# Turning nine of twenty normalized blocks by DMA, and a re-planned order, in a two-layer linear-attention and gated-MLP kernel

## The chip, the cores and the metric

One core of a Trainium2 chip runs the whole program. TensorE (PE in the profile) multiplies, VectorE (DVE) and ScalarE (ACT) read its results out of PSUM, GpSimd (POOL) works on SBUF alone, and SyncE (SP) and ScalarE issue the DMAs. The metric is the device time of one execution in microseconds (us). Less is better.

## The reference

`x` is 2048 rows of 512 in bf16. Two layers follow one another with the same weights; each adds an attention part A and a gated part B to `x`, each behind a layer normalization without weights:

```python
qkv = (x @ wqkv).reshape(B, S, 3, H, Dh)          # H = 32 heads of Dh = 16
pq, pk = q @ w_phi, k @ w_phi                      # per head, 16 x 16
phi_q = concat([softmax(pq), softmax(-pq)])
phi_k = concat([softmax(pk), softmax(-pk)])
kv, z = phi_k^T @ v, sum(phi_k)                    # sums over all 2048 rows
A = ((phi_q @ kv) / (phi_q @ z + 1e-6)) @ wo
B = (relu(x @ W_gate) * (x @ W_up)) @ W_down       # 1376 wide
```

No row of an attention output can be made before `kv` and `z` are summed over all rows.

## The kernel before

**Tiling.** The 2048 rows are 16 tiles of 128 rows, taken in five blocks of 2, 4, 4, 4 and 2 tiles (`SLABS`). Layer L (0 or 1) and block s have a normalization for part A, called `aLs`, and one for part B, called `gLs`: twenty in all.

**Stages of a block.** `layernorm` takes the statistics of each tile on VectorE (line 730, 731), makes the factor on ScalarE as exp(-0.5 ln) (733, 735), applies it on VectorE (750) or ScalarE (747) into `ytile`, and turns rows into columns, `yT`, which is what all following matmuls read. Two ways of turning exist: one tile at a time (`tr`, line 612) where `STEPS` says so, and else `strips` (line 775): four PSUM banks, 16 matmuls of 32x32 blocks a tile against an identity, and four evictions from PSUM by VectorE (690) or ScalarE (693). `keys` makes `expk` = exp(+-k) (803), its sums `Zk` (805), the reciprocal `rZk` (807), `vhat` = v times the reciprocal (815) on GpSimd or VectorE, and the products `kv` (827). `queries` makes `expq` (871). `attend` makes denominators (886 to 902), spreads the result over the partitions, either through TensorE (973, blocks 0 and 1) or through a scratch in device memory (DMAs of lines 912 and 916, blocks 2 to 4), scales `expq` by it (958, 988, 991), forms the numerators (928) and multiplies by `wo`. `glu` is part B; its outputs are added to `x_sb` at line 995.

**The order.** The program is recorded as a list of operations with a cost each. `Program.schedule` then places them: at each step it takes, among the operations whose inputs are ready, the one with the earliest start less a bonus (`BONUS`, by stage), and among those the lowest place in the list less a lead (`LEAD`, by stage). `ENG` says which engine takes an operation that more than one could do. The result is one fixed order for each engine, with semaphore waits between engines; at run time an engine executes its list in order and waits where its next operation isn't ready. The planner's costs decide the order and nothing else: they hold no engine up at run time. An operation with `port=True` is kept by the planner from lying beside a GpSimd operation.

**Queues.** SP issues the loads, then the scratch DMAs, then the stores of the output, in one list; ScalarE issues two key weight loads and one small one at the start.

Of the kernel before, what the change touches and what calls it, by code (L numbers as in the profile page):

```python
# [20 lines left out]
LEAD = {'': 1581,  # L21
 'at00': -9,
 'at01': -1074,
 'at02': -507,
 'at03': -757,
 'at10': -335,
 'at11': 762,
 'at12': -656,
 'at13': 331,
 'at14': -567,  # L30
 'd00': -5820,
 'd01': -1699,
 'd02': -13878,
 'd03': -2622,
 'd04': 3155,
 'd10': -13359,
 'd11': -2460,
 'd12': -1931,
 'd13': 71,
 'd14': -310,  # L40
 'fk': -480,
 'gl00': -2522,
 'gl01': 1205,
 'gl02': -5857,
 'gl03': -1218,
 'gl04': 504,
 'gl10': -2926,
 'gl11': -481,
 'gl12': -7344,
 'gl13': -46,  # L50
 'gl14': -166,
 'k00': 4572,
 'k01': 869,
 'k02': 459,
 'k03': -281,
 'k04': -136,
 'k10': 388,
 'k11': -124,
 'k12': -1352,
 'k13': 414,  # L60
 'k14': -1,
 'la00': -523,
 'la01': -375,
 'la02': 9240,
 'la03': 2125,
 'la04': -103,
 'la10': -743,
 'la11': -3565,
 'la12': -1372,
 'la14': 7230,  # L70
 'lg00': 199,
 'lg01': -221,
 'lg02': 153,
 'lg04': -687,
 'lg11': -282,
 'lg12': -264,
 'lg13': 794,
 'lg14': 2775,
 'nm00': 842,
 'nm01': 32,  # L80
 'nm02': 3263,
 'nm03': -579,
 'nm04': 406,
 'nm10': -741,
 'nm12': 16,
 'nm13': -1558,
 'nm14': -3291,
 'q00': 5078,
 'q01': -515,
 'q02': -692,  # L90
 'q03': 3551,
 'q04': -1249,
 'q10': -241,
 'q11': -69,
 'q12': -281,
 'q13': -2355,
 'q14': -138,
 'sp00': 803,
 'sp01': 206,
 'sp02': 643,  # L100
 'sp03': 36,
 'sp04': 2026,
 'sp10': 11,
 'sp11': -275,
 'sp12': -193,
 'sp13': -604,
 'sp14': 1242,
 'su0': -202,
 'su1': -6,
 'wo00': -564,  # L110
 'wo01': -1486,
 'wo02': -805,
 'wo03': -998,
 'wo04': 84,
 'wo10': 477,
 'wo11': 1154,
 'wo12': -216,
 'wo13': -222,
 'wo14': -8,
 'z00': -275,  # L120
 'z01': -232,
 'z02': -28,
 'z03': -803,
 'z04': 287,
 'z10': -247,
 'z11': 1911,
 'z12': 85,
 'z13': -5,
 'z14': 170}
BONUS = {'': 400,  # L130
 'at00': 1500,
 'at01': 400,
 'at02': 200,
 'at03': 200,
 'at04': 200,
 'at10': 400,
 'd03': 200,
 'd11': 800,
 'd12': 200,
 'fk': 400,  # L140
 'fq': 200,
 'gl03': 200,
 'gl04': 200,
 'gl11': 200,
 'gl12': 1500,
 'k12': 200,
 'la00': 400,
 'la01': 200,
 'la13': 200,
 'lg10': 400,  # L150
 'nm00': 200,
 'nm04': 200,
 'q11': 200,
 'sp00': 200,
 'sp01': 200,
 'sp03': 200,
 'sp10': 400,
 'sp11': 200,
 'sp13': 200,
 'su0': 800,  # L160
 'su1': 1500,
 'wo04': 400,
 'wo10': 400,
 'wo13': 200,
 'wo14': 200,
 'z03': 200,
 'z04': 200,
 'z10': 200,
 'z12': 400,
 'z13': 200}  # L170
HOLD = {}
ENG = {'ap/a00/0': 'act',
 'ap/a01/0': 'dve',
 'ap/a01/1': 'dve',
 'ap/a01/3': 'dve',
 'ap/a02/0': 'dve',
 'ap/a02/3': 'dve',
 'ap/a03/0': 'dve',
 'ap/a10/1': 'act',
 'ap/a11/1': 'act',  # L180
 'ap/a12/1': 'act',
 'ap/a12/2': 'act',
 'ap/a13/0': 'act',
 'ap/a13/3': 'act',
 'ap/a14/1': 'act',
 'ap/g01/0': 'act',
 'ap/g01/1': 'act',
 'ap/g01/3': 'act',
 'ap/g02/0': 'act',
 'ap/g02/3': 'act',  # L190
 'ap/g11/0': 'act',
 'ap/g12/2': 'act',
 'ap/g13/0': 'act',
 'ap/g13/2': 'act',
 'ap/g13/3': 'act',
 'ap/g14/1': 'act',
 'em/01/00': 'act',
 'em/01/01': 'dve',
 'em/01/02': 'act',
 'em/11/02': 'act',  # L200
 'em/11/03': 'dve',
 'fck3': 'act',
 'ftk0': 'dve',
 'ftq2': 'dve',
 'ftq3': 'dve',
 'ot/00/1': 'act',
 'ot/00/3': 'act',
 'ot/01/1': 'dve',
 'ot/01/2': 'dve',
 'ot/01/3': 'dve',  # L210
 'ot/02/1': 'dve',
 'ot/02/2': 'dve',
 'ot/02/3': 'dve',
 'ot/03/3': 'dve',
 'ot/04/1': 'dve',
 'ot/04/2': 'dve',
 'ot/04/3': 'dve',
 'ot/10/2': 'dve',
 'ot/11/1': 'dve',
 'ot/13/0': 'dve',  # L220
 'ot/14/0': 'dve',
 'ot/14/1': 'dve',
 'ot/14/2': 'dve',
 'vc/0/5': 'dve',
 'vc/0/6': 'dve',
 'vc/1/0': 'dve',
 'vc/1/12': 'dve',
 'vc/1/2': 'dve',
 'vc/1/5': 'dve',
 'vc/1/6': 'dve',  # L230
 'vc/1/7': 'dve',
 'vc/1/8': 'dve',
 'vc/1/9': 'dve',
 'vh/0/10/1': 'dve',
 'vh/0/13/1': 'dve',
 'vh/0/15/0': 'dve',
 'vh/0/15/1': 'dve',
 'vh/0/7/0': 'dve',
 'vh/0/9/0': 'dve',
 'vh/1/0/1': 'dve',  # L240
 'vh/1/1/0': 'dve',
 'vh/1/10/0': 'dve',
 'vh/1/14/1': 'dve',
 'vh/1/15/0': 'dve',
 'vh/1/15/1': 'dve',
 'vh/1/3/1': 'dve',
 'vh/1/4/1': 'dve',
 'vh/1/5/0': 'dve',
 'vh/1/8/1': 'dve',
 'yc/a01/01': 'act',  # L250
 'yc/a01/03': 'act',
 'yc/a02/00': 'act',
 'yc/a02/03': 'act',
# [3 lines left out]
 'yc/a04/1': 'dve',  # L257
 'yc/a10/00': 'dve',
 'yc/a10/02': 'dve',
 'yc/a11/03': 'act',  # L260
 'yc/a12/01': 'act',
 'yc/a12/03': 'act',
 'yc/a13/00': 'dve',
# [3 lines left out]
 'yc/g01/03': 'act',  # L267
 'yc/g02/00': 'dve',
 'yc/g04/00': 'dve',
 'yc/g04/02': 'dve',  # L270
 'yc/g04/03': 'act',
 'yc/g10/0': 'dve',
 'yc/g10/1': 'dve',
 'yc/g11/02': 'dve',
 'yc/g11/03': 'act',
 'yc/g12/01': 'act',
 'yc/g13/02': 'dve',
 'yc/g14/02': 'dve',
 'yc/g14/03': 'act'}
# [29 lines left out]
class Op:  # L309
    __slots__ = ("idx", "eng", "fn", "reads", "writes", "occ", "lat", "name", "is_dma", "nbytes",  # L310
                 "deps", "odeps", "users", "missing", "ready", "start", "finish", "cnt", "stream", "prio", "bonus", "port")

    def __init__(self, idx, eng, fn, reads, writes, occ, lat, name, is_dma=False, nbytes=0):
        self.idx, self.eng, self.fn = idx, eng, fn
        self.reads, self.writes = list(reads), list(writes)
        self.occ, self.lat, self.name = float(occ), float(lat), name
        self.is_dma, self.nbytes = is_dma, nbytes
        self.deps, self.odeps, self.users = set(), set(), []
        self.missing, self.ready = 0, 0.0
        self.start = self.finish = self.cnt = self.stream = None  # L320
        self.prio = idx
        self.bonus, self.port = 0.0, False


class Program:
# [4 lines left out]
    DMA_BW = 270.0  # L330

# [4 lines left out]
    def op(self, eng, fn, reads=(), writes=(), occ=100.0, lat=None, name="", bonus=0.0, port=False):  # L336
        o = Op(len(self.ops), eng, fn, reads, writes, occ, occ + 100.0 if lat is None else lat, name)
        o.bonus, o.port = bonus + BONUS.get(self.tag, 0.0), port
# [5 lines left out]
    def dma(self, eng, fn, reads=(), writes=(), nbytes=0, name=""):  # L344
        o = Op(len(self.ops), eng, fn, reads, writes, self.DMA_ISSUE[eng], 0, name, True, nbytes)
        o.bonus = BONUS.get(self.tag, 0.0)
        o.prio -= LEAD.get(self.tag, 0)
        self.stages.setdefault(self.tag, []).append(o)
        self.ops.append(o)
        return o  # L350
# [42 lines left out]
    def schedule(self):  # L393
        self.derive()
        free = {e: 0.0 for e in ENGINES}
        qfree = ported = 0.0
        ready = {e: [] for e in ENGINES}
# [9 lines left out]
        while left:  # L407
# [25 lines left out]
            for b in new_banks(o):  # L433
# [4 lines left out]
                if old is not None:  # L438
                    for x in old.ops:
                        if x.eng != "pe":  # L440
                            o.deps.add(x.idx)
            o.start = s
            if o.port:
# [3 lines left out]
            if o.is_dma:  # L447
# [3 lines left out]
                o.finish = qfree + 0.65 * self.DMA_LAT  # L451
# [75 lines left out]
def build_kernel(nc, A_x, A_wqkv, A_w_phi, A_wo, W_gate, W_up, W_down, out):  # L527
# [8 lines left out]
    with ExitStack() as ctx:  # L536
# [96 lines left out]

        load_x(0, 1)
        load_x(1, 2)
        dma("act", lambda e: e.dma_start(wphi[:], A_w_phi.rearrange("(kc hl) d f -> (hl d) kc f", hl=8)),
            writes=[R("wphi")], nbytes=131072, name="ld wphi")
        for c in (0, 2):
            dma("act", (lambda c: lambda e: e.dma_start(Wknat[:, c:c + 2, :], wqkv_v[:, c:c + 2, 512:1024]))(c),
                writes=R_Wnat["k"][c:c + 2], nbytes=262144, name="ld wk")  # L640
# [18 lines left out]
        op("dve", lambda e: e.memset(ones, 1.0), writes=[R("ones")] + [R("yT", NYT - 1, i) for i in range(4)], occ=480, name="ones")  # L659
# [5 lines left out]
        for i in range(NWARM):  # L665
            op("pe", lambda e: e.matmul(full(warm), ones[:, 0:128], ones[:, 0:512], start=True, stop=True),
               reads=[R("ones"), R("yT", NYT - 1, 0)], writes=[warm], occ=427, lat=640, name="warm")
        op("pool", lambda e: e.affine_select(ident[:], ones[:, 0:128], [[1, 128]], ALU.is_equal, 0.0, base=0, channel_multiplier=-1),
           reads=[R("ones"), R("yT", NYT - 1, 0)], writes=[R("ident")], occ=260, name="ident")
        op("pool", lambda e: e.affine_select(mask8a[:], ones[:, 0:8], [[-16, 8]], ALU.is_ge, 0.0, base=0, channel_multiplier=1),  # L670
           reads=[R("ones"), R("yT", NYT - 1, 0)], writes=[R("mask8a")], occ=150, name="mask8a")
# [48 lines left out]
        def layernorm(key, st, steps):  # L720
# [4 lines left out]
            for gi, step in enumerate(steps):  # L725
# [12 lines left out]
                if "act" in engs:  # L738
                    op("dve", (lambda t0, step: lambda e: e.scalar_tensor_tensor(nmr[:, t0:t0 + step, :], mv[:, t0:t0 + step, 0:1], -1.0, rstd[:, t0:t0 + step, :], ALU.mult, ALU.mult))(t0, step),  # L739
                       reads=Rmv + Ry, writes=[R("nmr", t) for t in ts], occ=75, lat=165, name="nmr")  # L740
                ybs = []
                for t, eng in zip(ts, engs):
# [6 lines left out]
                    else:  # L749
                        op("dve", (lambda t, yb: lambda e: e.tensor_scalar(ytile[:, yb, :], x_sb[:, t, :], mv[:, t, 0:1], rstd[:, t, :], op0=ALU.subtract, op1=ALU.mult))(t, yb),  # L750
                           reads=[R("x", t), R("mv", t), R("rs", t)], writes=[R("y", yb)], occ=322, lat=405, name=f"apply{t}", port=True)
                r0 = t0 - first[st]
                if step > 1:
# [10 lines left out]
        def strips(key, gi, b, r0, ybs):  # L764
# [13 lines left out]
            op("pe", turn, reads=[R("y", yb) for yb in ybs] + [R("ident")], writes=pss, occ=150 + 112 * m, lat=350 + 112 * m, name=f"ytr{key}")  # L778
# [7 lines left out]
        def keys(L, st, b):  # L786
# [3 lines left out]
            for tt in range(nt):  # L790
# [11 lines left out]
                for s in range(2):  # L802
# [4 lines left out]
                op("dve", (lambda zb, rz: lambda e: e.reciprocal(rZk[:, rz, :], Zk[:, zb, :]))(zb, rz),  # L807
                   reads=[R("Zk", zb)], writes=[R("rZk", rz)], occ=420, lat=534, name=f"rZk{t}")
# [4 lines left out]
                for s in range(2):  # L813
# [3 lines left out]
                       reads=[R("vsb", vb), R("vsb1"), R("rZk", rz)], writes=[R("vh", i, s)], occ=1060 if eng == "pool" else 630, lat=1130 if eng == "pool" else 730, name=f"vh{t}")  # L817
# [15 lines left out]
            for js in KVS[nt]:  # L833
                op("pe", products(js), reads=[R("ek", tiles[j], sg) for j in js for sg in range(2)] + [R("vh", tiles[j], sg) for j in js for sg in range(2)],
                   writes=[ps], occ=60 + 220 * len(js), lat=260 + 220 * len(js), name=f"kv{st}")
            flat = kvsum[:].rearrange("p g n -> p (g n)")
            if st == 0:
# [3 lines left out]
                   reads=[R("kvs")], writes=[R("kvs")], occ=70, lat=160, name="eps z")  # L841
# [3 lines left out]
        def sums():  # L845

            kvv = kvsum[:].rearrange("p g (h e) -> p g h e", e=17)
            for s in range(2):
# [3 lines left out]
                   reads=[R("kvs"), R("mask8")], writes=[R("ZD")] if s else [R("ZD"), R("ZD0")], occ=100, lat=190, name="zdw")  # L852
# [283 lines left out]
```

## Time and profile before

| what | value |
|---|---|
| median of 3 runs | 412.19 us (410.04 to 414.71) |
| the profiled execution | 414.23 us |
| its span, first to last instruction | 412.5 us |
| granted TensorE clock over the span | 0.992 |
| VectorE, ScalarE, GpSimd busy | 293.2, 209.5, 56.2 us |
| HBM read and written | 13.68 and 2.42 MB |

The span is what the profile describes; 1.73 us of the profiled execution lie outside it. The profiled execution is 2.04 us above the median. Busy times are sums over a span whose stages have different limits, so the prediction reads them by stretches. A matmul's shown duration includes its way through the array, and consecutive ones overlap; the distance from one to the next, not the duration, is its cost.

### The profile page before, as it was taken

To read this page: it belongs to the slowest core of one execution; us is meant where nothing else is said; L and a number is where in the kernel's file an instruction comes from. 1 tells how busy PE (TensorE), PEld (TensorE's weight loads), DVE (VectorE), ACT (ScalarE), POOL (GpSimd) and SP (SyncE) were. 2 spreads that over 40 slices of the span, in tenths; PEclk is the share of its full clock that TensorE was granted. 3 is DMA by queue.
4 is the path that set the end of the run, shared out by engine and by line. 5 is a ranking of instruction groups with operands and counts; after the bars stand their busy time and mean duration, and the time that the engine had idled before them with its cause. 6 is when DMAs were issued, how large, how long until landed. Compare 5 with 4: busy or idle time off the path is not lost.

```text
span 412.5 us, 11244 instructions
## 1 busy us (share of the span) xinstructions
PE 396.0 (96%) x4879; PEld 208.4 (51%) x4879; DVE 293.2 (71%) x586; ACT 209.5 (51%) x434; POOL 56.2 (14%) x55
## 2 busy tenths in 40 slices
PE   6899997999999998999999999999999999999997
PEld 3544543564444444445445745557444444444475
DVE  4899998897367779793988489638996354762253
ACT  4998998455304772247421477987335213432220
POOL 0068670000000232000600027000000000000000
PEclk9999998999999999999999999999999999999999
DMA  8960000300000003000100000011320000010011
GB/s 269 338 217 3 3 2 5 108 4 0 2 0 2 2 5 107 2 2 5 52 2 2 2 2 3 9 53 56 112 66 13 27 27 1 13 40 2 0 35 43
DMA packets 17922, 16.83 MB, mean 41 GB/s; under 512 B 3056, under 2 KB 16848, under 8 KB 17872
## 3 DMA queue, kind: packets, MB, share of 16 engines
q1 hardware_dynamic: 16656, 15.50, 11.6%
q8 instruction: 38, 0.62, 0.6%
q10 hardware_dynamic: 1216, 0.61, 0.5%
q14 instruction: 12, 0.10, 0.1%
HBM read 13.68 MB, written 2.42 MB: 39 GB/s over the span
## 4 chain that ended last, share of the span: by engine, by line
PE 79%; DVE 13%; ACT 3%; DMA 2%; issue 1%; POOL 1%; ACTq 0%; DVEq 0%
PE pb L608 72%; DVE Zk L805 3%; PE pb L886 2%; DVE vhat L815 2%; PE pb L775 2%; PE pb L827 2%; DMA hT<-in_A_wqkv_dram 1%; DVE stats L730 1%; DVE rZk L807 1%; PE pb L928 1%; DMA abT<-spread 1%; ACT expk L803 1%; PE pb L612 1%; DVE expq L991 1%; DVE vsb L690 1%
## 5 line engine op out<-in xcount | busy, mean ns | idle before, releaser
L1018 ACT ACTIVATE gate_sb<-pb 128x512 bf16<-128x512 f32 (+2 forms) x90 | 52.8, 587 | 113.0 <-PE pb L608 112.9
L1020 DVE TENSOR_TENSOR hT<-gate_sb,pb 128x512 bf16<-128x512 bf16 (+2 forms) x90 | 59.7, 670 | 64.5 <-PE pb L608 62.9
L608 PE MATMUL pb<-yT,Wu 128*128 128x512 bf16 (+3 forms) x440 | 94.6, 337 | 0.0
L608 PE MATMUL pb<-yT,Wg 128*128 128x512 bf16 (+3 forms) x440 | 92.6, 337 | 0.0
L815 POOL TENSOR_TENSOR vhat<-vsb,rZk 128x544 bf16<-128x544 bf16 x48 | 55.3, 1177 | 197.8 <-DVE rZk L807 116.6
L608 PE MATMUL pb<-Wd,hT 128*128 128x512 bf16 (+2 forms) x363 | 81.2, 373 | 0.0
L608 PEld LDWEIGHTS pb<-yT,Wg 128*128 128x128 bf16 (+1 forms) x440 | 43.2, 100 | 32.9 <-issue 0.7
L608 PEld LDWEIGHTS pb<-yT,Wu 128*128 128x128 bf16 (+1 forms) x440 | 43.1, 100 | 31.8 <-issue 0.6
L995 DVE TENSOR_TENSOR x_sb<-x_sb,pb 128x512 bf16<-128x512 bf16 x59 | 39.2, 680 | 22.8 <-PE pb L608 22.6
L608 PEld LDWEIGHTS pb<-Wd,hT 128*128 128x128 bf16 (+1 forms) x363 | 34.8, 98 | 39.4 <-issue 0.8
L803 ACT ACTIVATE expk<-pb 128x512 bf16<-128x512 f32 x64 | 35.4, 621 | 10.2 <-PE pb L608 8.8
L730 DVE BATCH_NORM_STATS2 stats<-x_sb 128x6 f32<-128x512 bf16 x60 | 39.4, 675 | 0.9 <-DMA x_sb<-in_A_x_dram 0.5
L805 DVE TENSOR_REDUCE Zk<-expk 128x64 f32<-128x1024 bf16 x32 | 37.6, 1189 | 1.7 <-ACT expk L803 1.6
L871 ACT ACTIVATE expq<-pb 128x512 bf16<-128x512 f32 x64 | 33.5, 623 | 6.1 <-PE pb L608 6.1
L608 PE MATMUL pb<-wv,yT 128*128 128x512 bf16 x128 | 34.5, 382 | 0.3 <-ACT expk L803 0.3
L608 PE MATMUL pb<-Wkp,yT 128*128 128x512 bf16 x128 | 34.1, 380 | 0.0
L608 PE MATMUL pb<-wo_sb,oT 128*128 128x512 bf16 x128 | 31.7, 392 | 0.8 <-ACT oT L693 0.8
L608 PE MATMUL pb<-yT,Wqp 128*128 128x512 bf16 (+1 forms) x160 | 31.6, 337 | 0.4 <-DVE yT L690 0.3
L693 ACT ACTIVATE yT<-pb 128x512 bf16<-128x512 bf16 (+1 forms) x36 | 19.5, 593 | 15.4 <-PE pb L775 14.4
L733 ACT ACTIVATE lnv<-mv,eps 128x4 f32<-128x4 f32 (+2 forms) x25 | 7.7, 307 | 34.7 <-DVE mv L731 34.2
L747 ACT ACTIVATE ytile<-x_sb,nmr,rstd 128x512 bf16<-128x512 bf16 x27 | 20.9, 815 | 1.4 <-DVE nmr L739 1.3
L608 PEld LDWEIGHTS pb<-wo_sb,oT 128*128 128x128 bf16 x128 | 12.2, 100 | 16.0 <-DVE oT L690 1.7
(77 smaller groups left out, 328.9 us busy)
## 6 DMA issues: line engine op xcount, KB each, us to landing
abT<-spread SPq DMA_DIRECT2D x32, 128.0 KB
out_dram<-x_sb SPq DMA_DIRECT2D x15, 128.0 KB, 4.0
x_sb<-in_A_x_dram SPq DMA_DIRECT2D x3, 512.0 KB
Wg<-in_B_W_gate_dram SPq DMA_DIRECT2D x1, 1376.0 KB
Wu<-in_B_W_up_dram SPq DMA_DIRECT2D x1, 1376.0 KB
Wd<-in_B_W_down_dram SPq DMA_DIRECT2D x1, 1280.0 KB
abT<-spread SPq DMA_DIRECT2D x16, 64.0 KB
hT<-in_A_wqkv_dram ACTq DMA_DIRECT2D x2, 256.0 KB
```

Of the source, the lines that this page charges most:

```text
L608: op("pe", lambda e: e.matmul(view(ps), lhsT, rhs, start=start, stop=stop), reads=reads, writes=[ps], occ=max(25.0, 0.4167 * n + 2.6), lat ...
L693: op("act", lambda e: e.activation(dst(), src(), ACT.Copy), reads=[ps] + reads, writes=writes, occ=115 + 0.714 * n, lat=240 + 0.714 * n, n ...
L730: op("dve", (lambda t, src: lambda e: e.bn_stats(stats[:, t, :], src()))(t, src), reads=[R("x", t) if ps is None else ps], writes=[R("st", ...
L747: op("act", (lambda t, yb: lambda e: e.activation(ytile[:, yb, :], x_sb[:, t, :], ACT.Identity, bias=nmr[:, t, :], scale=rstd[:, t, :]))(t ...
L775: ins = e.transpose(pss[i].b16()[:, n0:n0 + 32], ytile[r, yb, c * 128:(c + 1) * 128], ident[r, r], tile_position=(32 * i, 0))
L803: op("act", (lambda i, s, pk: lambda e: e.activation(expk[:, i, s, :], full(pk), ACT.Exp, scale=1.0 - 2.0 * s))(i, s, pk), reads=[pk], wri ...
L805: op("dve", (lambda i, zb: lambda e: e.tensor_reduce(Zk[:, zb, :], expk[:, i, :, :].rearrange("p s (h f) -> p (s h) f", f=16), AX.X, ALU.a ...
L815: op(eng, (lambda i, s, vb, rz: lambda e: e.tensor_tensor(vhat[:, i, s, :, :], vsb[:, vb, :, :], rZk[:, rz, s * 32:(s + 1) * 32].unsqueeze ...
L871: op("act", (lambda c0, s, ps: lambda e: e.activation(eqv(st)[:, c0:c0 + per, s, :], ps.f32()[:, 0:per * n].rearrange("p (c n) -> p c n", ...
L995: op("dve", lambda e: e.tensor_tensor(x_sb[:, t, :], x_sb[:, t, :], full(ps), ALU.add), reads=[R("x", t), ps], writes=[R("x", t)], occ=597 ...
L1018: op("act", (lambda m, gb, pg, k: lambda e: e.activation(gate_sb[0:m, gb, 0:k], pg.f32()[0:m, 0:k], ACT.Relu))(m, gb, pg, k), reads=[pg], ...
L1020: op("dve", (lambda m, gb, hb, pu, k: lambda e: e.tensor_tensor(hT[0:m, hb, 0:k], gate_sb[0:m, gb, 0:k], pu.f32()[0:m, 0:k], ALU.mult))(m, ...
```

## The change

- `XPOSE` names nine normalizations: a11, a12, a13, g02, g03, g12, g13 (four tiles each), g04 and g14 (two each). For these `strips` isn't called; each tile of `ytile` is turned by one DMA from SBUF to SBUF, issued by SP, straight into `yT`.
- The first two key weight loads go ahead of all but the first tile of x, one on ScalarE's queue and one on SP's; the second tile of x and the small `w_phi` load come behind them.
- 14 of 32 reciprocals `rZk` are made on ScalarE as exp(-ln), two operations, in place of one on VectorE.
- In blocks 2 to 4 ten of the 24 scalings of `expq` (line 958) are done by GpSimd; before, VectorE did all.
- `vhat`: 30 of 64 on VectorE (before 16), 34 on GpSimd (before 48).
- The planner: VectorE operations with two inputs in SBUF are marked `port=True` and so kept from lying beside GpSimd's; a switch between kinds of TensorE work is booked at 95 ns; costs of several TensorE operations are changed; an SBUF turn is booked with `XISSUE` on SP and `XDELAY` behind it. `LEAD`, `BONUS` and `ENG` are all new, so the order changes on every engine.
- A bookkeeping repair: readers of the `ones` tile name the same resources as its writer.

```diff
+XPOSE = ('a11', 'a12', 'a13', 'g02', 'g03', 'g12', 'g13', 'g04', 'g14')
+XISSUE = 1500.0
+XDELAY = 2500.0
...
+    SWITCH = 95.0
...
+            if o.eng == "pe" and o.mode != mode:
+                s = max(s, free["pe"] + self.SWITCH)
...
         load_x(0, 1)
-        load_x(1, 2)
+        load_wk("act", 0)
+        load_wk("sp", 2)
         dma("act", lambda e: e.dma_start(wphi[:], A_w_phi.rearrange("(kc hl) d f -> (hl d) kc f", hl=8)),
             writes=[R("wphi")], nbytes=131072, name="ld wphi")
-        for c in (0, 2):
...
+        load_x(1, 2)
...
-                if step > 1:
+                if key in XPOSE:
+                    for j, yb in enumerate(ybs):
+                        dma("sp", (lambda r, yb: lambda e: e.dma_start(yT[:, b, :, r * 128:(r + 1) * 128], ytile[:, yb, :], transpose=True))(r0 + j, yb),
+                            reads=[R("y", yb)], writes=R_yT(b, r0 + j), nbytes=131072, name=f"ytx{t0 + j}", issue=XISSUE, delay=XDELAY)
+                elif step > 1:
                     strips(key, gi, b, r0, ybs)
...
+                    op("act", (lambda zb, rz: lambda e: e.activation(rZk[:, rz, :], Zk[:, zb, :], ACT.Ln))(zb, rz), reads=[R("Zk", zb), R("tables")], writes=[R("rZk", rz)], occ=165, lat=265, name=f"lZk{t}")
+                    op("act", (lambda rz: lambda e: e.activation(rZk[:, rz, :], rZk[:, rz, :], ACT.Exp, scale=-1.0))(rz), reads=[R("rZk", rz)], writes=[R("rZk", rz)], occ=165, lat=265, name=f"rZk{t}")
...
+            eng = ENG.get(f"es/{L}{st}/{c}", "dve")
+            t = 64 + 1.06 * n if eng == "dve" else 120 + 3.95 * n
+            op(eng, lambda e: e.tensor_tensor(part, part, abT[:, c].rearrange("p (s n) -> p s n", s=2)[:, :, 0:n], ALU.mult),
+               reads=Re + [R("abT", c, s) for s in range(2)], writes=Re, occ=t, lat=t + 91, name=f"em{st}", port=eng == "dve")
```

## The prediction

> **What bounds the kernel now.** I read the page first for the engine that carries the span.
>
> ```profile
> PE 396.0 (96%) x4879; PEld 208.4 (51%) x4879; DVE 293.2 (71%) x586; ACT 209.5 (51%) x434; POOL 56.2 (14%) x55
> ...
> PE 79%; DVE 13%; ACT 3%; DMA 2%; issue 1%; POOL 1%; ACTq 0%; DVEq 0%
> ```
>
> The chain of work that ended last is TensorE for four fifths. How close TensorE is to its own pace there is read from the chain in order of time (start, length, what):
>
> ```profile
> 91.25 0.59 PE pb L775 x64
> ...
> 153.24 0.72 DVE vhat L815
> 153.96 2.26 DVE Zk L805 x2
> 156.22 0.53 DVE rZk L807 x2
> 157.01 1.44 DVE vhat L815
> ...
> 335.09 27.96 PE pb L608 x129
> ```
>
> 27.96 us for 129 matmuls is 0.217 us each: in the GLU stretches TensorE never waits, and only work taken from it shortens them. A four-tile turning is 0.59 us. Around 150 us the chain leaves TensorE and runs through VectorE's key work. Where TensorE has holes, busy time by stretches shows (columns: stretch, then busy us and instructions of PE, PEld, DVE, ACT, POOL, granted clock, DMA share, GB/s):
>
> ```profile
> 50.00:61.50 11.50, 10.64 (x262) 5.51 (x260) 11.07 (x15) 11.02 (x23) 7.99 (x7) 1.00 0.01 1
> 61.50:69.40 7.90, 5.18 (x227) 2.88 (x217) 6.08 (x18) 6.21 (x16) 0.00 (x0) 1.00 0.02 4
> 69.40:77.20 7.80, 7.00 (x70) 2.51 (x70) 6.46 (x17) 5.07 (x14) 0.00 (x0) 0.78 0.12 35
> 77.20:112.80 35.60, 35.60 (x305) 20.70 (x302) 26.82 (x55) 16.88 (x31) 0.00 (x0) 1.00 0.08 26
> ...
> 149.20:161.00 11.80, 10.33 (x129) 4.74 (x130) 11.66 (x16) 6.28 (x13) 6.01 (x5) 1.00 0.24 77
> ...
> 249.00:270.40 21.40, 20.33 (x535) 11.73 (x529) 16.55 (x36) 17.47 (x43) 6.38 (x5) 1.00 0.05 14
> ```
>
> The reader is to see two kinds of hole. At 50 to 61.5 and 149 to 161 VectorE is full and GpSimd busy beside it (TensorE short by 0.9 and 1.5 us; with 1.1 in the last row, 3.5 us that faster VectorE work could close). At 61.5 to 77.2 nobody is full: the first block's denominators, scaling, numerators and normalization follow one another (TensorE short by 2.7 + 0.8 us), and after that the granted clock falls to 0.78 of the stretch, which over 7.8 us is another 1.7 us.
>
> **The change part by part.** Two more views give prices: instructions of one tile (min/median/max), and groups of instructions, one wait (us, times, longest) and a DMA row of the timeline.
>
> ```profile
> L815 POOL TENSOR_TENSOR vhat<-vsb,rZk x48: 1098/1103/1662, 23.6 to 253.8; 128x544 bf16<-128x544 bf16 x48
> L815 DVE TENSOR_TENSOR vhat<-vsb,rZk x16: 709/1144/1666, 40.5 to 254.3; 128x544 bf16<-128x544 bf16 x16
> ```
> ```profile
> L693 ACT ACTIVATE yT<-pb 128x512 bf16<-128x512 bf16 x33 | 18.5, 613 | 8.6 <-PE pb L775 7.6 <-PE pb L612 0.9
> ...
> L958 DVE TENSOR_TENSOR expq<-expq,abT 128x1024 bf16<-128x1024 bf16 x16 | 10.9, 681 | 0.4 <-DMA abT<-spread 0.4
> ```
> ```profile
> PE pb L612 <- DMA hT<-in_A_wqkv_dram: 2.4, 1, 2.4
> ```
> ```profile
> 74.65 2.47 SPq L916 DMA_DIRECT2D abT<-spread  x4
> ```
> ```profile
> out_dram<-x_sb SPq DMA_DIRECT2D x15, 128.0 KB, 4.0
> ```
>
> *Turning leaves TensorE.* Seven four-tile turnings at 0.59 us and two two-tile ones at 0.30 (chain, 366.12) are 4.7 us, all in stretches where TensorE is the path: -4.7 us. With them go 36 evictions: 15 of 0.613 and 3 of 0.382 us on ScalarE (10.3 us), 13 of 0.411 and 5 of 0.279 on VectorE (6.7 us). In GLU stretches these lie beside TensorE and are worth nothing by themselves.
>
> *What replaces it.* 32 DMAs of 128 KB on SP. No turn by DMA is in the trace. The nearest row of the same size on the same queue is abT: 2.47 us for four, 0.62 us each; a 128 KB store lands after 4.0 us. If a turn held its queue until it has landed, it would cost 4.0. So t, the queue's time for one turn, lies between 0.62 and 4.0 us, and the last of four is there 4t + 3.4 us after the first is issued (4.0 less 0.62 is 3.4). It could also gain: four turns at 0.62 are ready about when 0.59 us of matmuls and a row of evictions would be, without four free PSUM banks; I count no gain, since TensorE rarely waited for those. Against this stands the room that the new order leaves, counted in the built program between the last matmul that feeds a normalization and the first that reads its `yT`: g03 63 matmuls (13.7 us at 0.217), g02 73 (15.8), g14 80 (17.4), g12 and g13 more. Feeding takes x_sb add 0.68, statistics 0.67 and 0.17, factor 0.32 + 0.23, nmr 0.22, apply 0.82: 3.1 us, and as VectorE needs 6.1 us for four tiles that TensorE delivers in 3.5, another 2.6. That leaves 8.0 us in g03 and 10.1 in g02, enough for t up to 1.15 and 1.7. In a12 tiles arrive every 11 matmuls (2.4 us), so it keeps pace to t of about 2.4; a13's four tiles come within 1.1 us, so feeding takes 7.3; from the last of them 12.0 us of matmuls stand before its first reader and 19.8 before its last, which leaves 4.7 for one turn (t up to 1.3) and 12.5 for four (2.3). At t = 1.5 TensorE is late by about 2 us in all, at 4.0 by 11.4 + 9.3 in g03 and g02, 6.9 in a13 and some 3 each in a11 and a12: 34 us. I take abT's 0.62 as nearest (same bytes, queue, SBUF target): 0, and keep +34 for the range. The turns also stand in SP's list before later scratch DMAs; eight of them put the next block's spread back by 8t, 5 us at 0.62, which the GLU matmuls hide; and a turn behind a spread that still waits for VectorE's aT is held with it.
>
> The Trainium skill has two rules here that disagree. "VectorE: DVE Perf Modes", The three transpose paths, gives 1309 ns for a 128x128 block by DMA against 390 on TensorE and advises TensorE; four blocks a tile would be, as an estimate, t = 5.2 us, and the sum almost 50 us worse. "Advanced Engine Details and Errata", X-Bar Transpose (TRN2), says such DMAs are about as fast as plain ones, and by it nothing is added. The trace cannot say.
>
> *Opening.* TensorE waits 2.4 us for the second key weight half. Now both halves are issued first, on two queues. Bounds 0 (VectorE, full from 20 us on, sets the pace) and -2.4; I take -1.5. The second x tile moves back behind them; its keys now stand later in TensorE's list, so nothing waits.
>
> *VectorE and GpSimd.* Lone `vhat` on VectorE takes 0.709 us, the median beside GpSimd 1.144. VectorE loses 14 reciprocals (7.4 us at 0.531), seven 128x1024 scalings (4.8), the evictions (6.7), and gets 14 `vhat` (9.9 at 0.709, 16.0 at 1.144); if the plan keeps the two apart, the old 16 shrink by 6.6 as well. It is 3 to 16 us lighter. Of the 3.5 us of holes where VectorE or the `vhat` chain is late I take 2.0 back; bounds 0 and -3.5. ScalarE gets 28 operations of about 0.26 us (7.3) for the 10.3 that it loses.
>
> *Scaling on GpSimd.* Seven of 128x1024, at 1.103 x 1024/544 = 2.08 us against 0.68 on VectorE, and three of half that. Numerators wait for the last of four scalings; three in a row on GpSimd (block 2, layer 1) take 6.2 us where VectorE needs 2.7 for four: up to 3.5 us late. GLU matmuls ahead of the numerators hide most; without that cover six stages cost up to 3.5 each. I take +1.0.
>
> *61.5 to 77.2.* The new order has eight query matmuls among this chain where there were seven, and the same steps: 0. Bounds: -1.7 (the slow clock goes) to +2 (another such hole). The planner's new costs change the order alone.
>
> Sum: -4.7 - 1.5 - 2.0 + 1.0 = -7.2. On the profiled execution's 414.23 that is 407.0; it stands 2.04 above the median, so 405.0.
>
> **The rivals.**
> *Holes close as well.* If VectorE really gets 16 us lighter, all 3.5 us of holes go, the opening gives 2.4 and the clock dip vanishes: -4.7 - 2.4 - 3.5 - 1.7 - 2 more of the chain at 61.5 to 69.4 = -14.3, 398. For: VectorE at 11.66 of 11.80 us. Against: the chain at 61.5 is of latencies, not load.
> *The saving is given back.* Turns at t of 1.5 to 2 make g03 and g02 late by 2 to 5 us, or the exclusion, which no semaphore enforces, does not hold and 30 `vhat` run at 1.144. Then 408 to 416; 411 as its middle. This is also the case in which the change doesn't do what it says.
> *The turning queue becomes the bound.* SP works in order; when t exceeds about 2.4, every group that takes tiles as they come falls behind. At t = 2.5: 5.4 in g03, 3.3 in g02, 3 in the others, 12 us: 417. At 4.0, 34 us: 439. The point from which it decides against the kernel before is where lateness passes 7.2 us, t of about 2.2. For: a turn moves 2-byte elements, unlike any row of the trace. Against: abT's issue pace.
>
> **How the numbers follow.** Forecast (401 to 408): 0.50. Holes close (394 to 401): 0.15. Given back (408 to 416): 0.15. Queue bound (over 416): 0.20. About 1% (4.1 us) is what a measurement of this kernel can tell from no change, so faster is below 408.1: 0.65; within: 0.15; slower: 0.20. The range 394 to 418 leaves out most of the last case and the far end of the second, under 2 in 10; the forecast's own is 401 to 408.
>
> **What would show it.** Line 775's matmuls from 864 to 352. The new SP rows give t directly: right if near 0.6 to 1.2, wrong above 2. TensorE waiting on a DMA into `yT` would be the new wait. `vhat` on VectorE near 0.71 shows the exclusion; the wait for the key weights under 1 us the opening; `expq` on GpSimd at 2.08 us, and numerators waiting for it, the scaling. The forecast is wrong if TensorE's holes in GLU stretches grow from none.

## The result, and the profile after

The changed kernel takes 409.01 us (median of 18 runs, 407.17 to 411.79) beside 412.72 (18 runs, 410.04 to 414.73): ratio 0.9915, 95% interval 0.9889 to 0.9941. The profiled execution is one of 407.92 us, span 406.2; the one of before had a span of 412.5. So the two profiles differ by 6.3 us and the medians by 3.7; both differences have to be explained. Medians and ratios below leave out three executions that took over 1.5% longer than the fastest of their kernel: 416.82 and 418.36 us in b_turn, and 579.34 us at a granted clock of 0.657, for a reason not known, in a_fill.

The page of after, its engines and the chain that ended last:

```profile
PE 381.1 (94%) x4310; PEld 204.3 (50%) x4367; DVE 286.4 (71%) x561; ACT 202.7 (50%) x440; POOL 59.6 (15%) x51
...
PE 76%; DVE 12%; ACT 5%; DMA 3%; issue 3%; SPq 1%; DVEq 0%
```

TensorE still carries the span, with 512 weight loads fewer (PEld had x4879). The strips that are left, then the turns by DMA and their time from issue to landing, each with minimum, median and maximum:

```profile
L862 PEld LDWEIGHTS pb<-ident,ytile x352: 90/90/94, 15.2 to 291.3; 32*128 32x128 bf16 x176
```
```profile
L838 SPq DMA_TRANSPOSE yT<-ytile x32: 1189/1266/1604, 118.6 to 367.8; - x32
```
```profile
DMA to landing us min/median/max: 2.4/2.5/2.7
```

The strips went from 864 weight loads to 352, as forecast. A turn holds SP's queue for 1.27 us, and its data lands 2.5 us after the issue. `vhat` in after:

```profile
L906 POOL TENSOR_TENSOR vhat<-vsb,rZk x34: 1097/1103/1661, 16.8 to 248.8; 128x544 bf16<-128x544 bf16 x34
L906 DVE TENSOR_TENSOR vhat<-vsb,rZk x30: 702/716/1619, 34.5 to 251.1; 128x544 bf16<-128x544 bf16 x30
```

VectorE's median fell from 1.144 to 0.716 us: the order does keep the two engines apart, for most of them.

**Where the time went.** The first matmul of the first gated part divides the run well: `pb<-yT,Wg` starts there. One tile's instructions, before and then after (the two starts are the first and the last):

```profile
L608 PEld LDWEIGHTS pb<-yT,Wg x440: 95/98/133, 79.0 to 403.8; 128*128 128x128 bf16 x134, 128*96 128x96 bf16 x13
```
```profile
L689 PEld LDWEIGHTS pb<-yT,Wg x440: 95/98/123, 80.6 to 397.5; 128*128 128x128 bf16 x134, 128*96 128x96 bf16 x13
```

Up to that matmul 79.0 us became 80.6; behind it 333.5 (412.5 - 79.0) became 325.6 (406.2 - 80.6), 7.9 less. By the chain's durations 4.7 of these are the strips. The durations leave out what stands around them; weight loads of before around one four-tile turning (start, length):

```profile
176.41 2.04 PEld L608 LDWEIGHTS pb<-Wd,hT 128*128 128x128 bf16 x10
...
179.46 1.19 PEld L608 LDWEIGHTS pb<-Wd,hT 128*128 128x128 bf16 x7
```

From 178.45 to 179.46 no load of part B runs, 1.01 us, where between two of them some 0.12 is usual (0.217 less 0.10): this turning takes 0.89 us, not 0.59. Read so, the nine come to about 7.1 us, an estimate. So the strips are 4.7 to 7.1 of the 7.9 and the new order 0.8 to 3.2. Closed holes don't show as much: TensorE's rows of waits behind that matmul add up to 2.8 us in before and, without the rows "issue", to 2.4 in after, though those for `vhat` fell from 2.3 to 0.4. Before that matmul it got worse. Busy time by stretches, until the sum over the keys is closed, first of before, then of after:

```profile
0.00:20.00 20.00, 14.77 (x166) 9.10 (x166) 13.39 (x43) 13.61 (x28) 0.84 (x7) 0.91 0.96 300
20.00:62.20 42.20, 40.53 (x864) 20.65 (x862) 41.51 (x72) 38.95 (x82) 28.91 (x26) 1.00 0.18 61
```
```profile
0.00:20.00 20.00, 13.71 (x154) 8.22 (x156) 15.66 (x43) 12.98 (x26) 3.00 (x9) 0.91 0.96 287
20.00:65.40 45.40, 38.66 (x858) 20.94 (x868) 43.03 (x71) 38.33 (x94) 23.55 (x20) 1.00 0.18 62
```

The third engine figure is VectorE: 41.51 of 42.20 us before, 43.03 of 45.40 after. With the first 20 us it works 54.9 us in before (13.39 + 41.51) and 58.7 in after (15.66 + 43.03), 3.8 more. By its groups of instructions the change took 5.1 us of reciprocals from it there, but the plan gave it 2.7 of casts of values, 1.9 of applies and 1.5 of `vhat`. TensorE's waits in the first 20 us of after, and then in all of it (us, times, longest):

```profile
PE pb L862 <- DVE hT L773: 2.2, 1, 2.2
PE pb L689 <- DVE stats L813: 1.6, 1, 1.6
```
```profile
PE pb L862 <- DVE vsb L773: 2.2, 1, 2.2
```

Two turnings of strips (12.7 and 38.2 us) now wait for VectorE, 2.2 us each. The stop for key weights, 2.4 us before, is no longer a row, and the first key matmul starts at 10.1 instead of 11.8.

### The profile page after: what moved, and what is told of

It is laid out like the page before. It is cut to its first block, busy times and chain, and to the rows that moved or that the text cites. A ratio compares the mean times of both kernels' runs of the same rounds, so it can differ in the third digit from the quotient of the medians.

```text
span 406.2 us, 10167 instructions
## 1 busy us (share of the span) xinstructions
PE 381.1 (94%) x4310; PEld 204.3 (50%) x4367; DVE 286.4 (71%) x561; ACT 202.7 (50%) x440; POOL 59.6 (15%) x51
## 2 busy tenths in 40 slices
DMA packets 35325, 20.96 MB, mean 52 GB/s; under 512 B 20464, under 2 KB 34256, under 8 KB 35280
## 3 DMA queue, kind: packets, MB, share of 16 engines
q1 hardware_dynamic: 34336, 19.96, 17.5%
## 4 chain that ended last, share of the span: by engine, by line
PE 76%; DVE 12%; ACT 5%; DMA 3%; issue 3%; SPq 1%; DVEq 0%
PE pb L689 71%; DVE Zk L892 3%; DVE vhat L906 2%; PE pb L977 2%; DMA x_sb<-in_A_x_dram 2%; ACT expk L890 1%; DMA abT<-spread 1%; PE pb L1019 1%; ACT expq L962 1%; PE pb L918 1%; DVE hT L1113 1%; PE pb L862 1%; ACT yT L776 1%; DVE ytile L833 1%; DVE rZk L895 1%
## 5 line engine op out<-in xcount | busy, mean ns | idle before, releaser
L1111 ACT ACTIVATE gate_sb<-pb 128x512 bf16<-128x512 f32 (+2 forms) x90 | 52.8, 588 | 123.6 <-PE pb L689 113.1
L689 PE MATMUL pb<-yT,Wg 128*128 128x512 bf16 (+3 forms) x430 | 95.5, 336 | 1.2 <-issue 0.5
L689 PE MATMUL pb<-Wd,hT 128*128 128x512 bf16 (+3 forms) x354 | 85.7, 372 | 0.5 <-DVE hT L1113 0.2
L906 POOL TENSOR_TENSOR vhat<-vsb,rZk 128x544 bf16<-128x544 bf16 x34 | 39.8, 1191 | 117.2 <-DVE rZk L895 82.3
L890 ACT ACTIVATE expk<-pb 128x512 bf16<-128x512 f32 x64 | 35.7, 599 | 12.9 <-PE pb L689 12.2
L962 ACT ACTIVATE expq<-pb 128x512 bf16<-128x512 f32 x64 | 33.5, 608 | 11.1 <-PE pb L689 10.7
L1051 POOL TENSOR_TENSOR expq<-expq,abT 128x1024 bf16<-128x1024 bf16 (+1 forms) x10 | 18.9, 1911 | 131.7 <-PE pb L689 125.7
L689 PE MATMUL pb<-Wkp,yT 128*128 128x512 bf16 x119 | 32.6, 386 | 3.1 <-DVE stats L813 1.6
L689 PE MATMUL pb<-yT,Wqp 128*128 128x512 bf16 (+1 forms) x149 | 29.2, 334 | 1.4 <-issue 1.1
L689 PE MATMUL pb<-wo_sb,oT 128*128 128x512 bf16 x124 | 29.4, 379 | 1.0 <-ACT oT L776 0.9
L906 DVE TENSOR_TENSOR vhat<-vsb,rZk 128x544 bf16<-128x544 bf16 x30 | 21.9, 768 | 0.1
L830 ACT ACTIVATE ytile<-x_sb,nmr,rstd 128x512 bf16<-128x512 bf16 x24 | 18.6, 806 | 3.2 <-DVE nmr L822 3.2
L689 PEld LDWEIGHTS pb<-Wkp,yT 128*128 128x128 bf16 x128 | 12.0, 99 | 16.2 <-DVE stats L813 1.8
```

The costliest lines, as they stand in the source:

```text
L689: op("pe", lambda e: e.matmul(view(ps), lhsT, rhs, start=start, stop=stop), reads=reads, writes=[ps], occ=max(25.0, 0.4167 * n + 2.6), lat ...
L830: op("act", (lambda t, yb: lambda e: e.activation(ytile[:, yb, :], x_sb[:, t, :], ACT.Identity, bias=nmr[:, t, :], scale=rstd[:, t, :]))(t ...
L890: op("act", (lambda i, s, pk: lambda e: e.activation(expk[:, i, s, :], full(pk), ACT.Exp, scale=1.0 - 2.0 * s))(i, s, pk), reads=[pk], wri ...
L906: op(eng, (lambda i, s, vb, rz: lambda e: e.tensor_tensor(vhat[:, i, s, :, :], vsb[:, vb, :, :], rZk[:, rz, s * 32:(s + 1) * 32].unsqueeze ...
L962: op("act", (lambda c0, s, ps: lambda e: e.activation(eqv(st)[:, c0:c0 + per, s, :], ps.f32()[:, 0:per * n].rearrange("p (c n) -> p c n", ...
L1051: op(eng, lambda e: e.tensor_tensor(part, part, abT[:, c].rearrange("p (s n) -> p s n", s=2)[:, :, 0:n], ALU.mult), reads=Re + [R("abT", c ...
```

## The experiments

In every kernel of this part the scheduler's choice is replaced by a written list, the one that it had made for the kernel before or for the changed one, so that an edit moves nothing else:

```diff
-        while left:
...
+        for o in map(keys.get, order):
+            s = max(free[o.eng], o.ready)
```

"Order of before" and "order of after" name these two lists. The ratios are against runs of the kernel before on the same chip; over three sets these have a median of 412.44 (63 runs) and a mean granted clock of 0.9953. The changed kernel's 18 runs have a mean of 0.9897. Distances between two kernels in us are between their medians, which come from different sets; where the intervals of their ratios overlap, the kernels are not told apart by time.

**The kernel before, once more (b_again).** No edit.

> The kernel before, unchanged. Theory A (the profiled pair differs by 6.3 us of span and the medians by 3.7 because executions differ in how many half-rate clock periods of 3.41 us they catch, each costing up to 1.7 us): times spread over about 4 us, and each execution's granted clock steps by about 0.004 with its time. Rival (the spread is noise without a cause in the profile): times and clocks are unrelated.

412.2 us (410.42 to 414.51, 10 runs), ratio 0.9989 (0.9959 to 1.002). The runs between 410.42 and 412.26 include clocks of 0.999 and 1.0, the slowest shows 0.992: part of the 4 us of spread comes with the clock. A straight line through time against clock gives 1.0 us for each 0.004 of clock in the 63 runs of before, and 1.3 in the changed kernel's 18.

**Turnings by DMA alone, in the order of before (b_turn).**

```diff
+XPOSE = ('a11', 'a12', 'a13', 'g02', 'g03', 'g12', 'g13', 'g04', 'g14')
...
-                if step > 1:
+                if key in XPOSE:
...
+                elif step > 1:
```

> The order of before, held fixed, with the nine turnings done by DMA, each issued right after its tile is normalized. Theory A (a turning by DMA takes 1.27 us of SP's queue a tile and lands 2.5 us after its start; it needs room that the new order gives and the old one does not): TensorE's list loses 4.7 us, but TensorE now waits before the first readers, so the time is no better than 411 and may be worse by several us. Rival (taking 4.7 us from TensorE pays whatever the order): about 408.

413.1 us, ratio 1.0019 (0.9985 to 1.0053). TensorE's own work fell by 4.7 us by the durations, and nothing was gained. The chain in order of time (start, length, what):

```profile
176.50 0.18 DVE stats L731
176.68 2.49 DMA yT<-ytile
179.17 0.14 issue
179.30 3.10 PE pb L609 x8
```

and TensorE's wait between 170 and 190 us:

```profile
PE pb L609 <- DMA yT<-ytile: 3.6, 1, 3.6
```

From the start of the last matmul that feeds this normalization (166.9) to the first gated matmul of block 3 of layer 0 (179.3) statistics, applies and four turns need 12.4 us, and the order of before has only 8.8 us of other matmuls there. TensorE stands 3.6 us, and the clock falls to half rate at 179.8. In the order of after the same distance is 15.8 us (165.9 to 181.7). Theory A holds: a turn by DMA needs room in the order.

**The same with g03 left on TensorE (b_turn8).** `XPOSE` without 'g03'.

> The order, the loads and the engines of the kernel before, with eight of the nine normalizations turned by DMA; the one that feeds g3 of layer 0 stays on TensorE, because in the run with nine g3 stood 4.0 us for its turned tiles. Theory (a turn gains its TensorE time wherever the order leaves about 5 us between the apply and its first reader): TensorE's own work falls by 8/9 of 4.7 = 4.2 us, the stop of 4 us at g3 is gone, and the time is 408 to 409.5 us beside 412.3, ratio 0.990 to 0.994. Rival (a stage that is bound by something other than TensorE takes the gain back wherever the turn is): 411.5 or more, ratio above 0.997.

408.97 us, ratio 0.9896 (0.9864 to 0.9928): as the theory had it. One turning of layer 1 still waits, 1.1 us at 357.7. Eight of the nine turnings, in the old order, gain as much as the whole change.

**The order of after, turned on TensorE (a_pe).** `XPOSE = ()`; the 32 tiles are turned by 4 transposes of 128x128 each and one eviction.

> The order of the changed kernel, held fixed, with the same 32 tiles turned on TensorE, tile by tile (four 128x128 turnings at 0.056 us each and one eviction a tile, VectorE and ScalarE in turn). Theory A (the gain after the first 80 us is TensorE time taken away): slower than the changed kernel by 7.2 us of TensorE time, 6 to 10 with late evictions: 415 to 419. Rival (the new order made the gain, and the turnings by DMA little): within 2 us of the changed kernel, under 411.

418.87 us, ratio 1.0144 (1.0095 to 1.0193). TensorE has 7.2 us more work (128 transposes at 0.056 us, as the chain's rows show them) and the time is 9.9 us above the changed kernel's. In the two profiles 7.2 us of it lie behind the first gated matmul; another 3.4 lie ahead, where the list is the same but this execution ran 13.7 us at half rate in place of 3.4. So what the new order gains, it gains with TensorE relieved.

**Old order of loads in the order of after (a_load).**

```diff
         load_x(0, 1)
+        load_x(1, 2)
...
+        load_wk("act", 0)
+        load_wk("act", 2)
```

> The order of the changed kernel, held fixed, but the loads in the old order (second tile of x ahead of the key weights, both halves on ScalarE's queue behind w_phi). Theory B (the earlier weights start the keys sooner, but VectorE's full list up to 65 us sets the end of that stage, so nothing is gained): within 0.7 us of the changed kernel. Rival (the prediction's step): slower by about 1.5 us.

413.6 us, ratio 1.0015 (0.9986 to 1.0043). Both were too low: it is 4.6 us above the changed kernel. TensorE's waits in its first 20 us show the loads' part:

```profile
PE pb L693 <- DMA hT<-in_A_wqkv_dram: 2.0, 2, 1.4
```

The first key matmul comes at 12.9 us, 2.8 later; at the first gated matmul it is 6.1 (86.7 for 80.6). The mean clock of the runs is 0.984, and the profile has half-rate periods at 44.1 and 74.8 us, the second 6.8 us long.

**First part of before, rest of after (hybrid).** Up to the first gated matmul of layer 0 the list, engines and loads of before; then the list of after.

> Everything up to the first GLU matmul of layer 0 in the order, on the engines and with the loads of the kernel before; everything after it as in the changed kernel, with its turnings by DMA. Theory (the change loses time in the first 80 us: 1.4 us more lost on TensorE there and about one more half-rate period of the clock, 1.7 us, and gains 3 us of holes and the TensorE time behind it): 405 to 407 us, that is 2 to 4 us under the changed kernel's 409.0, TensorE's lost time 20 to 21 us in the profile, and clocks of the runs 0.988 or more as in the runs of the kernel before. Rival (the half-rate periods and the first stage don't matter, or the later order only works behind its own first stage): 409 us or more.

404.27 us (402.58 to 405.77, 6 runs), ratio 0.9782 (0.9746 to 0.9818): 4.7 us under the changed kernel, more than expected. Its span is 404.0 with the clock at 1.000, and the division reads:

```profile
L527 PEld LDWEIGHTS pb<-yT,Wg x440: 95/98/123, 78.5 to 395.3; 128*128 128x128 bf16 x134, 128*96 128x96 bf16 x13
```

78.5 and 325.5 us. The later order's whole gain is there without its first part.

**The opposite (rev).** First part of after, rest of before.

> The opposite of the run called hybrid: everything up to the first GLU matmul of layer 0 in the order, on the engines and with the loads of the changed kernel; everything after it as in the kernel before, with all normalizations turned on TensorE. Theory (the two parts add: the new first stage costs 409.0 - 404.3 = 4.7 us whatever follows): 416.5 to 418.5 us beside 412.8, mean clock about 0.990. Rival (the first stage is only late because it was ordered to feed the new later order, and the old order absorbs it): 412 to 414 us.

426.32 us, ratio 1.0358 (1.0308 to 1.0409), beyond both. The chain shows that the seam is at fault:

```profile
86.61 2.21 DMA spread<-aT
...
90.75 3.17 DMA abT<-spread
...
94.01 0.69 DVE expq L889
```

The old list has block 2's numerators right behind, and in the old first part the denominators and their copies to scratch are already out; in the new one they are not. TensorE waits 7.0 us at 91 and then runs 6.8 us at half rate. The run can't say whether the parts add.

**Six casts of values back to ScalarE (a_vc).** Order of after.

```diff
- 'vc/0/0': 'dve',
...
- 'vc/0/8': 'dve',
```

> The changed kernel with its order, except that six casts of values (vsb) of layer 0's first stage are on ScalarE instead of VectorE. Theory 1 (VectorE, busy 43.0 of 45.4 us between 20 and 65.4 us, sets the end of the first attention stage): some 2.7 us leave VectorE, kv4 of layer 0 comes 1.5 to 2.7 us earlier, and the time is 406 to 407.5 us. Theory 2 (the holes there are of latency and order, not of VectorE's load): within 1 us of 409.0. Rival 3 (ScalarE is as full): 1 to 2 us slower than 409.0.

408.42 us, ratio 0.9881 (0.9842 to 0.9919). VectorE's work up to the end of the key sums falls by 4.1 us, from 58.7 to 54.6, and the sums end 2.2 us earlier (62.8 instead of 65.0), as theory 1 said. The time is 0.6 lower, which is theory 2's, but the interval overlaps the changed kernel's, so time doesn't decide; this profile has a second half-rate period, at 70.1 us, in the stage behind.

**Reciprocals back on VectorE (a_rz).** Order of after; 14 single operations in place of 28 on ScalarE.

> The changed kernel with its order, except that the 14 reciprocals that it computes on ScalarE in two steps are each one operation on VectorE again, at the place of the first step. Theory (VectorE's list sets the first attention stage): ten of them lie there, 0.42 us each by the others' duration, 2 to 4 us more: 411 to 413 us. Rival 1 (the stage's stops are of latency and order): 408.5 to 409.8 us. Rival 2 (ScalarE, relieved of 28 operations, is what the evictions wait for): 407 to 408.3 us.

414.64 us, ratio 1.0065 (1.0039 to 1.009): 5.6 us above the changed kernel, more than the theory's bound. VectorE's `rZk` take 0.542 us each, ten of them in the first stage. The key sums end at 69.6; up to 67.2 the stretch reads

```profile
20.00:67.20 47.20, 39.55 (x698) 20.19 (x705) 45.94 (x76) 32.94 (x72) 24.04 (x20) 0.93 0.17 60
```

VectorE 45.94 of 47.20. Ten more reciprocals are 5.4 us, and the sums end 4.5 us later; but this execution also ran 10.2 us of the stage at half rate (from 16.4 and 53.9), where the changed kernel's had 3.4, so how much of the delay is VectorE's own isn't shown.

**Scalings back on VectorE (a_es).** Order of after, the ten 'es' entries of `ENG` from 'pool' to 'dve'.

> The changed kernel with its order, except that the ten scalings of exponentials (expq times rZ) that it gave to GpSimd are on VectorE again. Theory (the prediction's term: on GpSimd they cost about 1 us): 408 to 409 us. Rival 1 (they relieve VectorE, which is the fuller engine): 410 us or more, since ten operations of about 1 us come back to it. Rival 2 (their 2.2 us beside VectorE's two-input operations block it): 407 us or less.

410.53 us, ratio 0.9953 (0.9927 to 0.9979): 1.5 above the changed kernel, rival 1, though the two intervals just overlap. They take 2.1 us on GpSimd and 0.68 on VectorE, and still GpSimd seems the better place; TensorE's waits from 240 to 300 us show one reason:

```profile
PE pb L862 <- DVE ytile L833: 1.4, 1, 1.4
```

A turning of strips of layer 1 now waits for an apply on VectorE, which has the scalings in its list ahead. A half-rate period follows at 295.5.

**Fillers (a_fill).** Order of after with 27 matmuls more.

```diff
+        def fill(ps, n):
+            for _ in range(n):
+                op("pe", lambda e: e.matmul(full(ps), ident[:], EC[:].rearrange("p c n -> p (c n)"), start=True, stop=True),
...
+                fill(pk, {'00': 7}.get(f"{L}{t}", 0))
...
+            fill(pss[0], {'a01': 10, 'a03': 10}.get(key, 0))
```

> The changed kernel with its order, plus 27 matmuls of 128x512 whose products are overwritten at once: 7 ahead of the first key matmul, 10 ahead of each of the two turnings of strips that waited 2.4 and 2.5 us (at 12.7 and 38.2 us). They only fill time in which TensorE stood still. Theory (stops of 2 us in the first 40 us let the clock fall to half rate for 3.4 us, in some runs more often than in others, and this makes the changed kernel's median 2 us worse than its order): mean granted clock of the runs 0.993 or more instead of 0.990, time 406.5 to 408 us. Rival 1 (the clock falls for other reasons, or costs nothing): clock 0.990 and 408.5 to 409.7 us. Rival 2 (the fillers come in the way): more than 409.7 us.

407.5 us (nine runs), ratio 0.9895 (0.9862 to 0.9927), with 5.8 us more TensorE work. The nine have a mean clock of 0.996. Two stretches of the changed kernel, then the same two with fillers (the figure after GpSimd's is the granted clock):

```profile
12.70:16.10 3.40, 1.19 (x76) 0.99 (x73) 3.26 (x8) 2.85 (x7) 0.00 (x0) 1.00 1.14 268
16.10:19.50 3.40, 3.18 (x18) 1.94 (x17) 3.05 (x9) 2.43 (x6) 2.16 (x2) 0.50 1.04 353
```
```profile
12.70:16.10 3.40, 3.40 (x87) 2.01 (x85) 3.30 (x8) 2.76 (x6) 0.00 (x0) 1.00 1.14 232
16.10:19.50 3.40, 2.87 (x55) 1.73 (x56) 3.34 (x10) 3.29 (x8) 2.16 (x2) 1.00 1.05 304
```

TensorE busy for 1.19 of 3.40 us is followed by 3.4 us at half rate; busy throughout, it is not. So the half rate follows the hole. Useless work in the holes made the kernel no slower: it is 1.5 us faster by the medians and 0.8 by the ratios, whose intervals overlap. The Trainium skill, "TensorE: Matmul & The Clock Gate", Part 1, describes a free-running window of 3413 ns and half rate after an idle one. The length agrees; here the window before was not idle but a third busy.

**New loads in the hybrid (h_load).**

```diff
         load_x(0, 1)
-        load_x(1, 2)
+        load_wk("act", 0)
+        load_wk("sp", 2)
```

> The run called hybrid (404.3 us), with the changed kernel's order of loads: the key weights ahead of the second x tile and the feature weights, the rest unchanged. Theory A (the prediction's step: the stop for the key weights, 1.9 us there, shrinks by 1.5 us): 402 to 403.3 us. Theory B (what follows in that order needs the second x tile and the feature weights as much): 404 to 405.5 us. Theory C (the load order is worth what it was worth in the changed order, 4.6 us): 399 to 401 us.

403.95 us (403.2 to 404.92, 6 runs), ratio 0.9806 (0.977 to 0.9843), not to be told from the hybrid's. Its first key matmul is at 9.9 us. The load order that is worth 4.6 us in the new first part is worth about nothing in the old one by these runs, nearest to theory B. With the hybrid it is the fastest version, 5 us under the changed kernel.

## Why the prediction was off

It said 405.0, a fall of 7.2 us; it was 409.0, a fall of 3.7. The main step that failed is "It is 3 to 16 us lighter", said of VectorE: up to the end of the key sums VectorE is 3.8 us heavier. One table divides the fourteen profiles (us; half-rate periods of the clock before the first gated matmul, by their start). The key sums end with the last weight load for `kv` in layer 0, in before and then in after (weight loads; chain):

```profile
61.14 0.36 PEld L827 LDWEIGHTS pb<-vhat,expk 128*32 128x32 bf16 x40 [0.89 <-issue]
```
```profile
61.18 0.38 PE pb L918 x32
...
62.02 0.66 PE pb L918 x64
...
64.89 0.22 PE pb L918 x7
```

In before the last 64 of these matmuls, block 4's, stand from 60.0 to 61.5; in after 128 are left at 61.18, with 64 others between block 4's two groups of 32. So the sums close at 61.5 and 65.0.

| kernel | first key matmul | from it to the end of the key sums | from there to the first gated matmul | span behind it | half rate at |
|---|---|---|---|---|---|
| before | 11.8 | 49.7 | 17.5 | 333.5 | 8.3, 69.7 |
| b_again | 9.9 | 49.4 | 17.6 | 333.8 | 67.4 |
| b_turn | 9.9 | 49.4 | 15.9 | 334.8 | none |
| b_turn8 | 11.1 | 49.5 | 15.9 | 329.9 | 8.1 |
| hybrid | 12.1 | 50.5 | 15.9 | 325.5 | none |
| h_load | 9.9 | 49.3 | 16.6 | 325.7 | 65.5 |
| after | 10.1 | 54.9 | 15.6 | 325.6 | 16.1 |
| a_es | 10.0 | 54.8 | 15.6 | 329.7 | 15.6 |
| a_vc | 9.9 | 52.8 | 17.1 | 326.6 | 15.5, 70.1 |
| a_fill | 10.0 | 53.4 | 16.1 | 325.1 | none |
| a_load | 12.9 | 55.6 | 18.2 | 325.4 | 44.1, 74.8 |
| a_pe | 10.3 | 55.5 | 18.3 | 332.8 | 10.7, 41.4, 72.2 |
| a_rz | 10.2 | 59.4 | 17.3 | 326.4 | 16.4, 53.9, 77.8 |
| rev | 10.2 | 55.5 | 18.0 | 343.6 | 10.1, 40.8, 71.5 |

Each period is 3.4 us long, those at 74.8, 72.2, 53.9 and 71.5 are 6.8. The part behind hardly varies where the list is the same (333.5 and 333.8; 325.1 to 325.7 in five kernels, with a_vc's 326.6 the exception); the first part varies by up to 3.7 us with the same list (first five rows: 79.0, 76.9, 75.3, 76.5, 78.5). Taking the profile's rear part and the 1.7 us outside the span from each median leaves an estimate of the median first part: before 412.4 - 333.5 - 1.7 = 77.2, hybrid 404.3 - 325.5 - 1.8 = 77.0, after 409.0 - 325.6 - 1.7 = 81.7. So the change is -7.9 behind and +4.5 ahead: -3.4, beside 3.7 measured against its own runs of before. The two profiles compared had a slow first part of before (two half-rate periods) and a good one of after (one), which is why they differed by 6.3.

Point by point:

- *Turning leaves TensorE, -4.7*: the way is right, the size is not settled. It adds durations, and distances between weight loads give about 7.1; b_turn8 shows 4.8 for eight turnings (333.6 - 329.9, and 1.1 of new wait). In the order of before the saving is lost where there is no room (b_turn) and gained where there is (b_turn8).
- *What replaces it, t = 0.62*: mis-sized, t is 1.27 us and the landing 2.5, but at no cost: TensorE waits for no turn in after. The limit that it counted for g03, 1.15, was a little too tight: the need is 12.4 us by b_turn, the room 15.8. The two rules of the Trainium skill quoted there missed on either side: 1.27 us for four blocks is 0.32 a block, not the 1309 ns of "VectorE: DVE Perf Modes", The three transpose paths, and twice the 0.62 of a plain DMA, not the same, as "Advanced Engine Details and Errata", X-Bar Transpose (TRN2), has it.
- *VectorE and GpSimd, -2.0*: "It is 3 to 16 us lighter" is true of the whole run (293.2 to 286.4, 6.8 us) and of the part behind the first gated matmul, where VectorE works 214.6 us for 224.2 and TensorE's waits for `vhat` fell by 1.9 us. It failed in the first stage, whose hole at 50 to 61.5 it was to close: its sum has reciprocals, scalings, evictions and `vhat`, but not the casts and applies that the new `ENG` and order put there, and it doesn't say where on the run each lies. From the first key matmul to the end of the key sums the old list takes 49.7 us (mean of five), the new one 54.9, and without its half-rate period, 1.7 at most (3.4 us at 0.50), 53.2: +3.5 (a_fill, with no such period, takes 53.4). The six casts are 2.1 of this (52.8 in a_vc's profile, with the same half-rate period). The other 1.4 stays open.
- *Scaling, +1.0*: probably the wrong sign, a gain of about 1.5 by a_es, whose interval and the changed kernel's just overlap. Numerators hardly wait for it, 0.4 us in all behind the first gated matmul, while VectorE's list had no room.
- *Opening, -1.5*: the first key matmul is at 9.9 to 10.3 us in eight profiles with the new loads and at 9.9 to 12.1, mean 11.0, in five with the old ones and the old order, so about -0.9. "Nothing waits" was wrong: TensorE stops 1.6 us ahead of the first key matmul. Its tile is evicted on ScalarE only at 9.42, behind three evictions of key weights, and VectorE stands 0.43 us for the second x tile, on which it starts at 8.86.
- *61.5 to 77.2, "the same steps: 0"*: right. From the end of the key sums to the first gated matmul, without a half-rate period, it is 15.9 us in the old list and 15.6 to 16.1 in the new one.
- *The clock, bound -1.7 as a gain*: it went the other way. From 0.9953 to 0.9897 is 0.0056, on 409 us 2.3 us of full pace, or 1.5 to 1.8 by the straight lines above; what is left of the +4.5 by the other steps, 4.5 + 0.9 - 3.5 + 0.3, is 2.2. Filling the holes brought the clock back to 0.996, so that the new holes lower the clock is shown; what this costs is an estimate, since the time moved by less than the intervals tell. Which of the holes set the clock back is shown only for the one at 12.7.

Of the rivals, the number fell into "the saving is given back", but by neither of its reasons: the turns were on time and the exclusion mostly held. It was given back in the first part, which had no turned tile in it; hybrid, with the old first part, shows this.

## What to carry to other kernels

A turn by DMA was a good trade here where the list had room for it: 15.8 us from the last feeding matmul to the first reader was enough, 12.4 was the need, of which 8.8 were covered in the old list. Test it in the old order, tile group by tile group, before re-planning. A re-planned order is to be judged stage by stage: here its first 80 us lost 4.5 and its last 325 gained 7.9, by estimate, and joining the better parts of the two lists gave 404.3. To divide two orders, take an event that ends the same work in both: the new list ends its key sums in another sequence. An engine's load is to be summed for each stage, over everything that moved. A stop of TensorE of 2 us can cost more than 2 us, since here the clock ran at half rate for 3.4 us behind one; a median over many runs, and their granted clocks, tell this, one profile doesn't.

## What was not expected of the hardware

- The half rate came after 3.4 us in which TensorE was still busy for a third (1.19 us, after, 12.7) or for more than half (1.92 us, before, from 66.3), and lasts 3.4 us or twice that. Between the end of the key sums and the first gated matmul it costs 1.6 to 1.7 us in the list of before (17.5 and 17.6 against 15.9), 0.7 in h_load.
- The same list reached its first key matmul at 9.9 to 12.1 us in five profiles. Two of the late ones have a half-rate period at 8 us; the latest has none, and TensorE waits 1.7 us there for weight DMAs.
- A turn of a 128x512 tile by DMA from SBUF to SBUF holds its queue for 1.27 us and lands after 2.5, with 32 of them raising the DMA packets from 17,922 to 35,325 without a visible wait.
